# Sum jobs on two hardware queues, raw weights loaded two steps ahead, and a new order in the cosine stage

## The chip, the cores and the metric

The kernel runs on one core of a Trainium2 chip. A core has a matrix engine (TensorE, PE in the profile; its weight loads are PEld), three engines for elementwise work (VectorE, DVE; ScalarE, ACT; GpSimd, POOL), a queue engine (SyncE, SP), and 16 DMA engines between its memory and the chip's. Each engine works through its own list of instructions in order and waits on semaphores. DMAs are started by an instruction on SP, ACT or POOL. The metric is the device time of one execution in microseconds (us).

## The reference

float32, with 2304 tokens (4 x 576), width 512:

```python
x = attention(q, k, v)        # 8 heads of 64; 4 with a window of 32, 4 with 32 positions at a stride of 4
h = x @ w_in                  # 512 -> 2048
r = np.maximum(h, 0.0)
x = (s * (r * r) + b) @ w_out # 2048 -> 512
h = x @ w2_in                 # 512 -> 2048
g = h * np.cos(h)
out = g @ w2_out              # 2048 -> 512
```

## The kernel before

**Numbers.** A float32 factor is split into a high part, rounded to what a fast matmul takes, and the low rest; a product is three matmuls (high x high, high x low, low x high). Splitting is one copy on ACT and one subtraction on DVE. The weights come in as 64-bit words and are converted to float32 on the chip (ACT `w_float`, DVE `w_join`).

**First MLP.** The tokens form five tiles (384, 384, 512, 512, 512). A step `p` is one tile t and one of 16 chunks of 128 of the 2048 hidden columns. In it PE computes the chunk's h (`mm_in`, 12 matmuls from the second tile on), ACT the squared relu, DVE the split g, and PE adds the chunk of two steps before to the output (`mm_out`, 12 matmuls; `LAG` is 2). Attention for later tiles, the conversion of the second MLP's weights and the jobs below are hung into the steps as events: `at((step, phase), ...)`, with `fire` called at three phases of a step. The engines' lists are written in exactly this program order.

**Weights of the second MLP.** 32 pieces are loaded raw (`w2_load`, SP), converted (`w2_float`, `w2_join`) and put back to memory (`w2_cut`): the 16 pieces of w2_out whole, the 16 of w2_in as high and low.

**Jobs.** The last product uses a two-by-two scheme with seven products (M1 to M7), for which the quarters of w2_out have to be combined first. This is done in eight jobs, from step 3 of the last tile on, each one and a half steps after the one before: `job_load` fetches two pieces (two DMAs of 256 KB), `job_sums` makes four sums on DVE, `job_split` splits the seven blocks (two ACT copies, two DVE subtractions) and stores them (two DMAs of 512 KB, two of 384 KB, in pieces of 1 KB). There are two buffers for jobs. Before the change all six DMAs of a job are issued by POOL.

**Second MLP.** It runs over 48 chunk steps n (three splits i of 768 tokens by 16 chunks). In a step PE computes the chunk's h into one of three banks (`mm_h`, 24 matmuls); then come `cos_n` (ACT), `cos_r` and `cos_q` (DVE; one part on ACT in later steps), and `cos_s` (ACT) and `cos_g` (DVE), which end the step before's chunk and so free its bank. `x_cut` splits a quarter of the next split's x. G is combined in place for the seven products; a unit (i, product, k) is 12 matmuls on a split operand (`unit_cut`) with loaded weights (`unit_load`). Units run one in steps 6, 10, 14, 18 and two in each of 27 later steps; the last 26 run after the last chunk. `evacuate` takes a finished product out of its bank.

Of the kernel before, what the change touches and what calls it, by code (L numbers as in the profile page):

```python
# [74 lines left out]
def attention_then_two_mlps(ctx, tc, qk_p, qk_d, v_p, v_d, mask_p, mask_d, w1, w2, sv, bv, out):  # L75
# [134 lines left out]
    def job_load(i):  # L210
        a = after_att[0].tile([P, 7, 256], F32, tag=f"job{i % 2}", name=f"job{i}")
        two = lambda fc: whole_out[fc].rearrange("p (e n) -> p e n", e=2)
        nc.gpsimd.dma_start(a[:, 0:6:5, :], two(2 * i))
        nc.gpsimd.dma_start(a[:, 4:7:2, :], two(2 * i + 1))
        jobs[i] = a
# [6 lines left out]
    def job_split(i):  # L222
        a = jobs.pop(i)
        for n, (lo, hi) in enumerate(((0, 4), (4, 7))):
            h, l = (
                wpool.tile([P, hi - lo, 256], F32R, tag=f"w{c}{2 * (i % 2) + n}", name=f"j{c}{i}_{n}") for c in "hl"
            )
            nc.scalar.copy(h, a[:, lo:hi, :])
            nc.vector.tensor_tensor(out=l, in0=a[:, lo:hi, :], in1=h.bitcast(F32), op=ALU.subtract)  # L229
            nc.gpsimd.dma_start(cut_out[:, lo:hi, i, 0, :], h.bitcast(F32))  # L230
            nc.gpsimd.dma_start(cut_out[:, lo:hi, i, 1, :], l.bitcast(F32))

# [360 lines left out]
    def unit_cut(u):  # L593
# [6 lines left out]
        split[u] = x  # L600
        if j == "M5" and not last:
            t2 = G[i, 0, k][:, 1]
            sub(t2, G[i, 1, k][:, 1], t2)
            ops[i, k, "M6"] = t2
            b11 = G[i, 0, k][:, 0]
            sub(b11, t2, b11)
            ops[i, k, "M7"] = b11
        if j == "M2" and last:
            t2 = home[0].tile([P, 2, SB], F32, tag=f"G{1 - i % 2}0{k}", name=f"t2_{k}")
            sub(t2, G[i, 1, k][:, 1], G[i, 0, k][:, 1])  # L610
            ops[i, k, "M6"] = t2
            b11 = G[i, 0, k][:, 0]
            sub(b11, t2, b11)
            ops[i, k, "M7"] = b11
        if j == "M2":
            b21 = G[i, 1, k][:, 0]
            sub(b21, b21, ops[i, k, "M6"])
            ops[i, k, "M4"] = b21

# [3 lines left out]
    def y_bank(i, j):  # L623
        if i < NS - 1 or j in ("M1", "M6", "M5", "M3"):
            if j in ("M1", "M2", "M7"):
                yy[i, "a"] = ps_o.tile([P, 2, 512], F32, tag="yy", name=f"yy{i}_{j}")
            return yy[i, "a"]
        if j in ("M2", "M7", "M4"):
            b = ps_h.tile([P, 2, 512], F32, tag=f"p{('M2', 'M7', 'M4').index(j) % 2}", name=f"yy{i}_{j}") if j != "M4" else (
                ps_o.tile([P, 2, 512], F32, tag="p2", name=f"yy{i}_{j}"))  # L630
            yy[i, j] = b
        return yy[i, j]
# [45 lines left out]
    def evacuate():  # L678
# [40 lines left out]
    with tc.manual_schedule():  # L719
# [128 lines left out]
        fresh_late = NP - NFC + BG_STEPS[-1][-1] + 2
        for cc in range(NCC):
# [86 lines left out]
        for n in range(1, NH):  # L936
# [119 lines left out]
```

## Time and profile before

| | |
|---|---|
| median of 2 runs | 933.95 us (933.94 to 933.96) |
| profiled execution | 935.2 us, span 933.4 us, granted PE clock 0.98 |
| PE busy | 888.3 us (95%) |
| DVE, ACT, POOL busy | 646.7, 540.9, 39.7 us |
| DMA | 173.09 MB, mean 185 GB/s |

The span is from the first to the last instruction of one profiled execution; its own time is slightly longer, and the median is that of executions without the profiler. A matmul's duration in the rows overlaps that of its neighbours, so the distance of two starts is what one costs. "Idle before <-X" in brackets is how long the engine stood still before the instruction, and what ended it.

### The profile page before, as it was taken

What the parts mean: (1) busy time and instruction counts of PE and PEld (TensorE: products, weight loads), DVE (VectorE), ACT (ScalarE), POOL (GpSimd) and SP (SyncE); (2) the same over time, 40 slices, a digit from 0 to 9 for tenths busy, and PEclk for the clock granted to TensorE, in tenths of its full rate; (3) what the DMA queues carried; (4) which work ended last, traced back from release to release, by engine and by line L of the source; (5) the groups of instructions that cost most, each with busy time, mean ns of one, the idle gap of its engine ahead of it and who ended that gap; (6) DMA issues with size and microseconds to landing.
All of it is one profiled execution on the core that took longest, in us unless ns stands there. A gap on an engine that the chain in (4) does not pass through costs nothing.

```text
span 933.4 us, 13908 instructions
## 1 busy us (share of the span) xinstructions
PE 888.3 (95%) x5148; PEld 788.6 (84%) x5148; DVE 646.7 (69%) x1063; ACT 540.9 (58%) x1079; POOL 39.7 (4%) x58
## 2 busy tenths in 40 slices
PE   8999999999999999999947979989999999999798
PEld 6666699998888888888836779989999999999798
DVE  6888887756554766768634459778677677666954
ACT  6777767766555555655423346546675666655533
POOL 1000000000000000100233300000000000000000
PEclk9999999999999999999978889999999999999999
DMA  9966235324533445456856594355666665665576
GB/s 261 335 235 208 70 123 152 95 96 151 166 119 114 165 165 178 136 185 226 311 214 202 190 351 147 113 181 179 183 199 212 196 183 183 203 212 157 172 243 207
DMA packets 62356, 173.09 MB, mean 185 GB/s; under 512 B 7153, under 2 KB 16849, under 8 KB 62289
## 3 DMA queue, kind: packets, MB, share of 16 engines
q1 hardware_dynamic: 56768, 153.13, 50.5%
q0 software_dynamic: 5376, 18.88, 5.8%
q8 instruction: 41, 0.67, 0.3%
q14 instruction: 27, 0.21, 0.1%
q10 hardware_dynamic: 144, 0.20, 0.1%
HBM read 135.48 MB, written 36.70 MB: 184 GB/s over the span
## 4 chain that ended last, share of the span: by engine, by line
PE 77%; DVE 8%; issue 6%; DMA 5%; ACT 2%; POOL 1%; SPq 1%; DVEq 0%; POOLq 0%
PE h L534 21%; PE yy_M L645 16%; PE h L425 5%; PE h L427 4%; PE h L426 4%; PE y L440 4%; PE y L441 4%; PE y L442 4%; PE y L437 4%; PE h L419 3%; PE sc L300 3%; DMA job<-whole_out 2%; PE pv L376 2%; PE tp L351 1%; DVE jl L229 1%
## 5 line engine op out<-in xcount | busy, mean ns | idle before, releaser
L534 PE MATMUL h<-x,wi 128*128 128x384 f32 x1152 | 209.8, 339 | 11.2 <-issue 11.2
L534 PEld LDWEIGHTS h<-x,wi 128*128 128x128 f32 x1152 | 203.9, 191 | 12.6 <-issue 12.4
L645 PE MATMUL yy_M<-op,wo 128*128 128x384 f32 x1008 | 183.1, 337 | 6.9 <-DVE op L599 5.0
L645 PEld LDWEIGHTS yy_M<-op,wo 128*128 128x128 f32 x1008 | 176.4, 189 | 9.3 <-DVE op L599 5.9
L440 PE MATMUL y<-g,wh 128*128 128x512 f32 (+1 forms) x256 | 101.5, 396 | 18.9 <-DVE g L497 18.9
L543 ACT ACTIVATE n<-h,pmagic 128x768 f32<-128x768 f32 x48 | 43.3, 902 | 114.7 <-PE h L534 107.1
L441 PE MATMUL y<-g,wh 128*128 128x512 f32 (+1 forms) x256 | 99.6, 389 | 0.2 <-DVE g L498 0.2
L442 PE MATMUL y<-g,wl 128*128 128x512 f32 (+1 forms) x256 | 99.0, 387 | 0.0
L425 PE MATMUL h<-xs,wh 128*128 128x512 f32 (+1 forms) x256 | 98.7, 386 | 0.0
L427 PE MATMUL h<-xs,wl 128*128 128x512 f32 (+1 forms) x256 | 96.4, 376 | 0.0
L426 PE MATMUL h<-xs,wh 128*128 128x512 f32 (+1 forms) x256 | 96.3, 376 | 0.0
L552 DVE SCALAR_TENSOR_TENSOR r<-n,h 128x768 f32<-128x768 f32 x48 | 45.8, 953 | 59.5 <-ACT n L548 51.8
L599 DVE TENSOR_TENSOR op<-G,op 128x768 fp32r<-128x768 f32 x80 | 74.4, 952 | 14.5 <-ACT op L598 14.5
L330 ACT ACTIVATE sm<-sm,nmax 96x80 f32<-96x80 f32 (+1 forms) x140 | 49.5, 355 | 49.5 <-DVE nmax L327 49.5
L598 ACT CAST op<-G 128x768 fp32r<-128x768 f32 x80 | 63.7, 828 | 22.5 <-PE yy_M L645 19.5
L440 PEld LDWEIGHTS y<-g,wh 128*128 128x128 f32 x256 | 50.1, 196 | 28.2 <-DVE g L497 20.6
L489 ACT ACTIVATE r<-h 128x512 f32<-128x512 f32 (+1 forms) x80 | 44.0, 550 | 45.2 <-PE h L427 40.3
L497 DVE CAST g<-r 128x512 fp32r<-128x512 f32 (+1 forms) x64 | 26.1, 407 | 51.9 <-ACT r L495 46.2
L570 DVE SCALAR_TENSOR_TENSOR G<-n,h 128x768 f32<-128x768 f32 x48 | 45.7, 953 | 19.5 <-ACT n L562 19.4
L441 PEld LDWEIGHTS y<-g,wh 128*128 128x128 f32 x256 | 49.9, 195 | 9.6 <-DVE g L498 1.9
L442 PEld LDWEIGHTS y<-g,wl 128*128 128x128 f32 x256 | 49.9, 195 | 8.0
L425 PEld LDWEIGHTS h<-xs,wh 128*128 128x128 f32 x256 | 48.1, 188 | 7.8
(108 smaller groups left out, 1323.9 us busy)
## 6 DMA issues: line engine op xcount, KB each, us to landing
wo<-cut_out SPq DMA_DIRECT2D x84, 512.0 KB, 4.2
wi<-cut_in SPq DMA_DIRECT2D x48, 512.0 KB, 5.3
stage<-w SPq DMA_DIRECT2D x32, 512.0 KB, 7.6
raw<-w SPq DMA_DIRECT2D x32, 512.0 KB, 5.0
qk<-qk_d SPq DMA_DIRECT2D x20, 352.0 KB, 3.4
qk<-qk_p SPq DMA_DIRECT2D x20, 304.0 KB, 3.1
x<-y SPq DMA_DIRECT2D x12, 384.0 KB, 6.2
out_t<-o SPq DMA_DIRECT2D x11, 384.0 KB, 3.0
```

Of the source, the lines that this page charges most:

```text
L330: nc.scalar.activation(out=sm[:, j, :], in_=sm[:, j, :], func=AF.Exp, bias=nmax[:, j : j + 1], scale=1.0, accum_out=ssum[:, j : j + 1],)
L425: nc.tensor.matmul(h[:, : SIZES[t]], hi, x[:, 0, :], start=cc == 0, stop=False)
L426: nc.tensor.matmul(h[:, : SIZES[t]], hi, x[:, 1, :], start=False, stop=False)
L427: nc.tensor.matmul(h[:, : SIZES[t]], lo, x[:, 0, :], start=False, stop=cc == NCC - 1)
L440: nc.tensor.matmul(y[:, : SIZES[t]], hi, g[:, 0, :], start=fc == 0, stop=False)
L441: nc.tensor.matmul(y[:, : SIZES[t]], hi, g[:, 1, :], start=False, stop=False)
L442: nc.tensor.matmul(y[:, : SIZES[t]], lo, g[:, 0, :], start=False, stop=fc == NFC - 1)
L534: nc.tensor.matmul(h[:, t, :SB], wt, x[:, t * SB : (t + 1) * SB], start=cc == 0 and k == 0, stop=cc == NCC - 1 and k == 2,)
L552: nc.vector.scalar_tensor_tensor(out=r, in0=v, scalar=-C1, in1=hp[n], op0=ALU.mult, op1=ALU.add)
L598: nc.scalar.copy(x[:, 0], src)
L599: nc.vector.tensor_tensor(out=x[:, 1], in0=src, in1=x[:, 0].bitcast(F32), op=ALU.subtract)
L645: nc.tensor.matmul(b[:, eb, :SB], wt, g, start=fresh and k == 0 and z == 0 and n == 0, stop=k == 3 and z == 1 and n == 2, skip_group_check ...
```

## The change

It moves the job's loads to SP, puts the stores of high parts on ACT and those of low parts on SP, and lets the load of job i + 2 follow the split of job i. Raw weights from the fifth piece on are loaded two steps ahead (phase 1) instead of one (phase 0). The three in-place sums of a split of G come one at a time, kept in a list `due` that `flush` works off later. In the last split the units of M1 and M2 are interleaved. From step 19 on a step first ends the chunk before (`cos_s`, `cos_g`, sums, `x_cut`) and then begins its own cosine. `x_cut` is in other steps, and operands are split as far ahead as the next steps' units need.

```diff
-LAST = ("M1", "M2", "M6", "M7", "M5", "M4", "M3")
+LAST = [("M1", k) for k in "012"] + [("M2", "0"), ("M2", "1"), ("M1", "3"), ("M2", "2"), ("M2", "3")]
+LAST += [(j, k) for j in ("M6", "M7", "M5", "M4", "M3") for k in "0123"]
...
     def job_load(i):
-        nc.gpsimd.dma_start(a[:, 0:6:5, :], two(2 * i))
-        nc.gpsimd.dma_start(a[:, 4:7:2, :], two(2 * i + 1))
+        nc.sync.dma_start(a[:, 0:6:5, :], two(2 * i))
+        nc.sync.dma_start(a[:, 4:7:2, :], two(2 * i + 1))
...
     def job_split(i):
-            nc.gpsimd.dma_start(cut_out[:, lo:hi, i, 0, :], h.bitcast(F32))
-            nc.gpsimd.dma_start(cut_out[:, lo:hi, i, 1, :], l.bitcast(F32))
+            nc.scalar.dma_start(cut_out[:, lo:hi, i, 0, :], h.bitcast(F32))
+            nc.sync.dma_start(cut_out[:, lo:hi, i, 1, :], l.bitcast(F32))
...
     def unit_cut(u):
-        if j == "M5" and not last:
-            t2 = G[i, 0, k][:, 1]
-            sub(t2, G[i, 1, k][:, 1], t2)
-            ops[i, k, "M6"] = t2
-            b11 = G[i, 0, k][:, 0]
-            sub(b11, t2, b11)
-            ops[i, k, "M7"] = b11
...
+        if j == ("M2" if last else "M5"):
+            due.append(lambda: sum_2(i, k))
+        if j == "M6":
+            due.append(lambda: sum_3(i, k))
+        if j == ("M7" if last else "M2"):
+            due.append(lambda: sum_4(i, k))
...
+    def flush():
+        while due:
+            due.pop(0)()
...
             elif j == "M5":
                 keep(i, "v", b)
-                sub(s["v"], s["v"], s["s"])
             elif j == "M6":
                 keep(i, "r", b)
+                sub(s["v"], s["v"], s["s"])
...
-            at((p - 1, 0), lambda k=k: w2_load(k))
+            at((p - 1, 0) if k < BG[1] else (p - 2, 1), lambda k=k: w2_load(k))
...
-            at((max(p - 2, NP - NFC), 2), lambda i=i: job_load(i))
+            if i < 2:
+                at((NP - NFC, 2), lambda i=i: job_load(i))
             at((p, 2), lambda i=i: job_sums(i))
             at((p + 1, 1), lambda i=i: job_split(i))
+            if i + 2 < NFC // 2:
+                at((p + 1, 2), lambda i=i: job_load(i + 2))
...
-        x_at = {5: (1, 0), 7: (1, 1), 9: (1, 2), 11: (1, 3), 22: (2, 0), 24: (2, 1), 26: (2, 2), 28: (2, 3)}
+        x_at = {6: (1, 0), 10: (1, 1), 12: (1, 2), 14: (1, 3), 24: (2, 0), 28: (2, 1), 29: (2, 2), 30: (2, 3)}
...
-            cos_n(n)
-            cos_r(n, n > 17)
-            cos_s(n - 1)
-            cos_g(n - 1)
-            cos_q(n)
-            if n in x_at:
-                x_cut(*x_at[n])
+            if n > 18:
+                cos_s(n - 1)
+                cos_g(n - 1)
+                flush()
+                if n in x_at:
+                    x_cut(*x_at[n])
+                cos_n(n)
+                cos_r(n, True)
+                cos_q(n)
+            else:
+                cos_n(n)
+                cos_r(n, n == 18)
+                cos_s(n - 1)
+                cos_g(n - 1)
+                cos_q(n)
+                flush()
+                if n in x_at:
+                    x_cut(*x_at[n])
...
-            cut_to(nu + 2)
+            ahead = at_unit.get(n + 1, 0)
+            cut_to(nu + ahead + (at_unit.get(n + 2, 0) if ahead < 2 else max(0, n + 3 - NH)))
...
         while nu < len(UNITS):
...
             evacuate()
+            cut_to(nu + 2)
+            flush()
             cut_to(nu + 3)
```

The order of the instructions at three places, before and in the change. Line numbers of the change are one or more higher. First the jobs: POOL's list around the load of the third job before (`job` is a job's buffer, `jh` and `jl` its high and low parts, `cut_out` the store).

```order
L213 DMA job_4501<-whole_out_111 128x2x256
L214 DMA job_4501<-whole_out_112 128x2x256
L230 DMA cut_out<-jh_0_4594 128x4x256
L231 DMA cut_out<-jl_0_4595 128x4x256
L230 DMA cut_out<-jh_1_4600 128x3x256
L231 DMA cut_out<-jl_1_4601 128x3x256
L213 DMA job_4610<-whole_out_113 128x2x256
L214 DMA job_4610<-whole_out_114 128x2x256
```

In the change SP's list at the stores of the third job's low parts and behind them.

```order
L232 DMA cut_out<-jl_0_4649 128x4x256
L232 DMA cut_out<-jl_1_4655 128x3x256
L214 DMA job_4660<-whole_out_115 128x2x256
L215 DMA job_4660<-whole_out_116 128x2x256
L517 DMA x_0_1_4703<-y_0_88 128x768
L517 DMA x_1_1_4706<-y_0_88 128x768
L517 DMA x_2_1_4709<-y_0_88 128x768
L517 DMA x_3_1_4712<-y_0_88 128x768
L232 DMA cut_out<-jl_0_4746 128x4x256
L232 DMA cut_out<-jl_1_4752 128x3x256
```

And ACT's list in the change at the fourth job, with the squared relu of steps 9 and 10 on either side.

```order
L490 ACTIVATE r_9_4727<-h_9_4714 128x512
L496 ACTIVATE r_9_4727<-r_9_4727 128x512
L229 CAST jh_0_4745<-job_4606 128x1024
L231 DMA cut_out<-jh_0_4745 128x4x256
L229 CAST jh_1_4751<-job_4606 128x768
L231 DMA cut_out<-jh_1_4751 128x3x256
L522 CAST x_0_0_4702<-x_0_1_4703 128x768
L490 ACTIVATE r_10_4779<-h_10_4766 128x512
```

The job's DMAs have moved from a list of their own into those of SP, among the loads, and of ACT, between casts and relus.

The second place is DVE's list at chunk steps 7 and 8 before (`n`, `r`: the cosine's tiles by chunk; `G`: the finished chunk; `op`: a split operand).

```order
L550 TENSOR_SCALAR n_7_5397<-n_7_5397 128x768
L552 SCALAR_TENSOR_TENSOR r_7_5400<-n_7_5397,h_7_5370 128x768
L570 SCALAR_TENSOR_TENSOR G_0_1_5313<-n_6_5345,h_6_5318 128x2x384
L580 TENSOR_TENSOR G_0_1_5313<-G_0_1_5313 128x768
L557 SCALAR_TENSOR_TENSOR n_7_5397<-n_7_5397,r_7_5400 128x768
L522 TENSOR_TENSOR x_1_1_5222<-x_1_1_5222,x_1_0_5221 128x768
L599 TENSOR_TENSOR op_5409<-G_0_1_5313,op_5409 128x768
L550 TENSOR_SCALAR n_8_5439<-n_8_5439 128x768
L552 SCALAR_TENSOR_TENSOR r_8_5442<-n_8_5439,h_8_5412 128x768
L570 SCALAR_TENSOR_TENSOR G_1_1_5352<-n_7_5397,h_7_5370 128x2x384
```

In the change:

```order
L551 TENSOR_SCALAR n_7_5397<-n_7_5397 128x768
L553 SCALAR_TENSOR_TENSOR r_7_5400<-n_7_5397,h_7_5370 128x768
L571 SCALAR_TENSOR_TENSOR G_0_1_5313<-n_6_5343,h_6_5316 128x2x384
L581 TENSOR_TENSOR G_0_1_5313<-G_0_1_5313 128x768
L558 SCALAR_TENSOR_TENSOR n_7_5397<-n_7_5397,r_7_5400 128x768
L551 TENSOR_SCALAR n_8_5434<-n_8_5434 128x768
L553 SCALAR_TENSOR_TENSOR r_8_5437<-n_8_5434,h_8_5407 128x768
L571 SCALAR_TENSOR_TENSOR G_1_1_5350<-n_7_5397,h_7_5370 128x2x384
L558 SCALAR_TENSOR_TENSOR n_8_5434<-n_8_5434,r_8_5437 128x768
L601 TENSOR_TENSOR op_5443<-G_0_1_5313,op_5443 128x768
```

The x part (L522) has left step 7, and the split (L599, L601 in the change) stands one step later.

The third place is DVE's list at the last chunk, 47, before (`t`: the sums of the last split).

```order
L552 SCALAR_TENSOR_TENSOR r_47_7900<-n_47_7897,h_47_7869 128x768
L570 SCALAR_TENSOR_TENSOR G_0_3_7763<-n_46_7825,h_46_7800 128x2x384
L580 TENSOR_TENSOR G_0_3_7763<-G_0_3_7763 128x768
L557 SCALAR_TENSOR_TENSOR n_47_7897<-n_47_7897,r_47_7900 128x768
L599 TENSOR_TENSOR op_7936<-G_0_2_7471,op_7936 128x768
L599 TENSOR_TENSOR op_7939<-G_0_3_7763,op_7939 128x768
L570 SCALAR_TENSOR_TENSOR G_1_3_7832<-n_47_7897,h_47_7869 128x2x384
L599 TENSOR_TENSOR op_7945<-G_1_0_6956,op_7945 128x768
L580 TENSOR_TENSOR t_0_7948<-G_1_0_6956,G_0_0_6919 128x768
L580 TENSOR_TENSOR G_0_0_6919<-t_0_7948,G_0_0_6919 128x768
L580 TENSOR_TENSOR G_1_0_6956<-G_1_0_6956,t_0_7948 128x768
L599 TENSOR_TENSOR op_7966<-G_1_1_7252,op_7966 128x768
```

In the change:

```order
L571 SCALAR_TENSOR_TENSOR G_0_3_7758<-n_46_7829,h_46_7800 128x2x384
L581 TENSOR_TENSOR G_0_3_7758<-G_0_3_7758 128x768
L553 SCALAR_TENSOR_TENSOR r_47_7907<-n_47_7904,h_47_7872 128x768
L558 SCALAR_TENSOR_TENSOR n_47_7904<-n_47_7904,r_47_7907 128x768
L571 SCALAR_TENSOR_TENSOR G_1_3_7827<-n_47_7904,h_47_7872 128x2x384
L601 TENSOR_TENSOR op_7942<-G_1_0_6951,op_7942 128x768
L601 TENSOR_TENSOR op_7945<-G_1_1_7244,op_7945 128x768
L581 TENSOR_TENSOR t_0_7962<-G_1_0_6951,G_0_0_6914 128x768
L581 TENSOR_TENSOR t_1_7964<-G_1_1_7244,G_0_1_7171 128x768
L601 TENSOR_TENSOR op_7966<-G_0_3_7758,op_7966 128x768
L601 TENSOR_TENSOR op_7984<-G_1_2_7538,op_7984 128x768
L581 TENSOR_TENSOR t_2_8001<-G_1_2_7538,G_0_2_7464 128x768
```

The G of chunk 46 stands in front of the cosine of chunk 47, and of the sums only `t` is left between the splits.

## Rows read from the trace of the kernel before

**Rows 1.** The page, section 1: busy time, share and instructions by engine.

```profile
PE 888.3 (95%) x5148; PEld 788.6 (84%) x5148; DVE 646.7 (69%) x1063; ACT 540.9 (58%) x1079; POOL 39.7 (4%) x58
```

**Rows 2.** Windows: length; PE, PEld, DVE, ACT, POOL busy; clock, DMA share, GB/s.

```profile
440.00:460.00 20.00, 20.00 (x90) 16.57 (x89) 18.16 (x32) 12.13 (x19) 6.03 (x8) 1.00 0.79 260
...
489.10:532.40 43.30, 36.09 (x133) 28.58 (x134) 22.25 (x36) 15.22 (x23) 15.22 (x21) 0.82 0.55 184
632.00:862.50 230.50, 229.23 (x1321) 228.50 (x1320) 165.86 (x183) 144.45 (x179) 0.00 (x0) 1.00 0.62 193
...
456.00:460.00 4.00, 4.00 (x19) 1.00 0.88 222
```

**Rows 3.** Timeline of PE, last tile: start, us, line, tiles; idle before.

```profile
466.39 0.39 PE L425 MATMUL h<-xs,wh 128*128 128x512 f32 x1
...
468.88 0.39 PE L427 MATMUL h<-xs,wl 128*128 128x512 f32 x1
476.37 0.79 PE L440 MATMUL y<-g,wh 128*128 128x512 f32 x1 [7.10 <-DVE g L497]
...
532.26 16.93 PE L534 MATMUL h<-x,wi 128*128 128x384 f32 x96
```

**Rows 4.** Waits: sum in us, count, longest in us.

```profile
PE y L440 <- DVE g L497: 18.9, 4, 7.1
...
ACT n L543 <- DMA cut_out<-jh: 7.6, 1, 7.6
```

**Rows 5.** Timeline of POOL at the third job.

```profile
482.21 0.73 POOL L213 DMA_DIRECT2D job<-whole_out  x1 [0.49 <-issue]
...
485.84 0.77 POOL L230 DMA_DIRECT2D cut_out<-jh  x1 [2.18 <-issue]
489.54 0.77 POOL L231 DMA_DIRECT2D cut_out<-jl  x1 [2.93 <-DVE g L497]
...
494.55 0.74 POOL L213 DMA_DIRECT2D job<-whole_out  x1 [0.53 <-issue]
```

**Rows 6.** DMA issues (KB, median us to landing); landings of L230.

```profile
y<-xy SPq DMA_DIRECT2D x2, 512.0 KB, 4.1
...
DMA to landing us min/median/max: 3.4/3.9/10.3
```

**Rows 7.** Timeline of SP and ACT queues: DMA issues.

```profile
418.51 1.21 SPq L462 DMA_DIRECT2D y<-xy  x2
...
548.13 7.37 SPq L516 DMA_DIRECT2D x<-y  x4
...
930.01 0.37 ACTq L669 DMA_DIRECT2D out_t<-o  x1
```

**Rows 8.** Chain of waits: start, us, what (`issue`: PE stands still).

```profile
549.21 5.31 issue
554.52 10.82 PE h L534 x48
...
579.93 1.29 issue
...
620.52 3.27 issue
...
631.87 4.16 PE h L534 x24
```

**Rows 9.** Timeline of DVE before the G at 580.18.

```profile
576.92 0.95 DVE L522 TENSOR_TENSOR x<-x,x 128x768 fp32r<-128x768 f32 x1
...
578.65 0.55 DVE L550 TENSOR_SCALAR n<-n 128x768 f32<-128x768 f32 x1
...
580.18 0.95 DVE L570 SCALAR_TENSOR_TENSOR G<-n,h 128x768 f32<-128x768 f32 x1
```

**Rows 10.** Chain of waits: PE's last chunk and last products.

```profile
858.36 4.17 PE h L534 x24
...
904.25 25.22 PE yy_M L645 x144
```

More of the change, by code (lines that the diff above doesn't have):

```diff
@@ L580, in sub @@
         nc.vector.tensor_tensor(out=out, in0=a, in1=b, op=ALU.subtract)
-    UNITS = [(i, j, k) for i in range(NS) for j in (PRODUCTS if i < NS - 1 else LAST) for k in range(4)]
+    UNITS = [(i, j, k) for i in range(NS - 1) for j in PRODUCTS for k in range(4)]
+    UNITS += [(NS - 1, j, int(k)) for j, k in LAST]
     cutn = [0]
@@ L600, in unit_cut, with sum_2, sum_3, sum_4 @@
         split[u] = x
-        if j == "M5" and not last:
-            t2 = G[i, 0, k][:, 1]
-            sub(t2, G[i, 1, k][:, 1], t2)
-            ops[i, k, "M6"] = t2
-            b11 = G[i, 0, k][:, 0]
-            sub(b11, t2, b11)
-            ops[i, k, "M7"] = b11
-        if j == "M2" and last:
-            t2 = home[0].tile([P, 2, SB], F32, tag=f"G{1 - i % 2}0{k}", name=f"t2_{k}")
[L610 to L618, printed above, removed]
+        if j == ("M2" if last else "M5"):
[4 more added lines that the diff above has]
+            due.append(lambda: sum_4(i, k))
+    due = []
+    def flush():
+        while due:
+            due.pop(0)()
+    def sum_2(i, k):
+        t2 = G[i, 0, k][:, 1]
+        if i == NS - 1:
+            t2 = home[0].tile([P, 2, SB], F32, tag=f"G{1 - i % 2}0{k}", name=f"t2_{k}")
+        sub(t2, G[i, 1, k][:, 1], G[i, 0, k][:, 1])
+        ops[i, k, "M6"] = t2
+    def sum_3(i, k):
+        b11 = G[i, 0, k][:, 0]
+        sub(b11, ops[i, k, "M6"], b11)
+        ops[i, k, "M7"] = b11
+    def sum_4(i, k):
+        b21 = G[i, 1, k][:, 0]
+        sub(b21, b21, ops[i, k, "M6"])
+        ops[i, k, "M4"] = b21
     yy = {}
@@ L623, in y_bank @@
     def y_bank(i, j):
[L624 to L632, printed above, removed]
+        if j in ("M5", "M6", "M3") or (j == "M4" and i < NS - 1):
+            return yy[i, "M7" if j == "M4" else "M1"]
+        place, tag = (ps_o, "yy")
+        if i == NS - 1 and j != "M1":
+            place, tag = {"M2": (ps_h, "p0"), "M7": (ps_h, "p1"), "M4": (ps_o, "p2")}[j]
+        return place.tile([P, 2, 512], F32, tag=tag, name=f"yy{i}_{j}")
     def unit(u):
@@ L636, in unit @@
         if k == 0:
-            yy[i, "now"] = y_bank(i, j)
-        b = yy[i, "now"]
+            yy[i, j] = y_bank(i, j)
+        b = yy[i, j]
         fresh = j in ("M1", "M2", "M7") or (i == NS - 1 and j == "M4")
@@ L683, in evacuate @@
         if i < NS - 1:
-            b = yy[i, "a"][:, :, :SB]
+            b = yy[i, j][:, :, :SB]
             if j == "M1":
@@ L701, in evacuate @@
             return
-        b = yy[i, "now"][:, :, :SB]
+        b = yy[i, j][:, :, :SB]
         if j == "M1":
```

## The prediction

> **What bounds the kernel now.** I read the page first: TensorE (PE) counts as busy for 95% of the span [rows 1], so a change can win little more than the idle remainder and what a lowered clock adds to it. Busy time by stretch comes next [rows 2]: from 632 to 862 us PE is busy 229.23 of 230.50 us at full clock, and nothing but PE counts there. In the last tile of the first MLP it is busy 36.09 of 43.30 us (489.1 to 532.4) at a granted clock of 0.82. Third I read PE's timeline and the waits [rows 3, 4]. The reader should see PE stop at 468.88 + 0.23 and start again at 476.37, waiting for DVE's g: four such waits, 18.9 us. DVE is idle then too; it stands in front of the sums of a job, whose raw weights are not yet loaded. POOL's timeline shows why [rows 5]: it issues loads and stores of the jobs one at a time, a store's two issues 3.70 us apart (485.84 to 489.54), and a job's six DMAs take 12.34 us (482.21 to 494.55). PE gives a job one and a half steps; from 466.39 to 468.88 eleven matmul starts take 2.49 us, so 0.227 us each, 24 matmuls and 5.44 us a step, **8.16 us** a job. POOL is the slower of the two, and the DMA engines are busy only 0.55 there [rows 2].
>
> **The sum, stretch by stretch.** The profiled execution's span is 933.4 us, its own time 935.2; the median of the runs, 933.95, is 0.55 above the span. I subtract from the span and add 0.55.
>
> *A, last tile, 469.1 to 532.4 us.* PE has left there seven output groups and four input groups of 12 matmuls (11 x 2.72 = 29.9 us) and one cosine chunk of 24 (4.16 us, [rows 8]): 34.1 us of work in 63.3 us [rows 3]. With the jobs off POOL up to **29.2 us** can go, slow-clock time included, since the difference is taken against full-speed work.
> What replaces it: 16 job loads and 16 stores of the low halves on SP, 16 stores of the high halves on ACT. Issue: the nearest row is the parked y, also 512 KB in pieces of 1 KB, 1.21 us for two on SP; the ends are 0.37 us (ACT's one store) and 1.84 us (four x loads in 7.37 us when the engines are full) [rows 7]. I take 0.6, by likeness: 1.2 us a job on ACT, 2.4 on SP. ACT is busy 15.22 of 43.30 us there [rows 2], 4.3 us per 12.34 us job, so 5.5 of 8.16 with the stores: hidden by PE. If that cover went, 8 x 1.2 = 10 us would show.
> On SP the job's load now stands behind the low stores of the job two before it, and these wait for DVE; behind them wait x and w_in loads. The load goes out about two steps (10.9 us) ahead of its sums, against landings of 3.9 median and 10.3 longest for POOL's stores and 4.1 for the parked y [rows 6]. So it lands just in time even in the longest case.
> Bytes: a job moves 2 x 256 + 2 x 512 + 2 x 384 KB = 2.36 MB. At 184 GB/s for a share of 0.55 the engines carry about 334 GB/s when full, an estimate from that row, so 7.1 us a job: under 8.16, not far. Jobs 3 to 7, four x and four w_in loads are 15.5 MB, 46.3 us, while steps 8 to 15 last 43.5. I therefore leave 3 us in (bounds 0 to 18, see the first rival): **-26.2**.
> DVE was the tightest engine before step 8 (18.16 of 20.00 us busy at 440 to 460, [rows 2]); nothing is added to it, and PE did not stall while it was so.
> A rule of the Trainium skill, "DMA: Bandwidth & Descriptors", section "Issuing engines are not separate DMA queues", speaks against this term: all queues share the same 16 engines, and issuing from several saves only issue time, which is usually small beside the transfer. The trace differs: engines at 0.55 while POOL paces them. By the rule the time would be that of the third rival, 918; by the row it is the one here.
>
> *B, 549.2 to 554.5 us.* PE waits 5.31 us for a bank [rows 8]; the cosine that frees it waited 7.6 us for the last job's store to leave its memory [rows 4]. Now that store goes out in step 15, before PE's last two output groups. The chain from the first cosine chunk to its freed bank is some 9 us and PE has three chunks (12.5 us) to do: **-5.3** (0 if the stores land 5 us late).
>
> *C, chunks 5 to 18, 554.5 to 631.9 us.* 77.35 us for 384 matmuls [rows 8] of 4.16/24 = 0.173 us: 66.6 us of work, 10.8 lost. One part is the slow clock after B's stop (48 matmuls in 10.82 instead of 8.32). The rest comes from three stops, two of 1.29 and one of 3.27 us: a chunk's bank is freed by DVE's G, and in the step before the G at 580.18 DVE also had a difference, an x part and a split to do [rows 9]. The change spreads them: x parts move to steps 6, 10, 12 and 14, three of which also run a product on PE (2.08 us more cover); splits move by one; the two in-place sums of a split leave step 15. A step has four fixed DVE instructions, 0.55 and three of 0.95 [rows 9], 3.4 of 4.16 us; one more of 0.95 now fits before the bank is due. I leave 1.8 us for steps with two extras: **-9.0** (bounds -10.8 to 0).
>
> *D, 632 to 862 us.* Doing a step's end before the new chunk's cosine moves DVE's G out from behind the wait for PE, but PE hardly waits: at most 1.27 us [rows 2]. I take **-0.6**. The move of one difference from M5 to M6 and the later sums cost nothing here: 8.32 us of PE a step cover them; without that cover it is the second rival.
>
> *E, the end.* From 862.53 to 929.47 us [rows 10] PE runs 28 products of 12 matmuls, 58.2 us at 0.173: 8.7 lost, most of it waiting for operands that DVE had not split. Three sums per M2 split (0.95 each) sat in DVE between two splits. Now the last G but one no longer waits for the last chunk, three M1 and two M2 products come before the late M1 product, and each split has one sum behind it: 1.9 us of DVE for 2.08 of PE. Following the new order, the first M2 split still comes about 1 us late, and two more about 0.5 each: 2 us stay, **-6.7** (bounds -8.7 to 0).
>
> *Weights two steps ahead.* The last 28 of the 32 raw loads go out more than a step earlier. Where the tile before them was stored in place, SP now waits for that store to land, and what is queued behind it (q and k loads, the next store) with it; these have whole steps of PE's work ahead of them. No wait of PE's names a raw load, so there is nothing to win or to lose: 0. Without that cover it would show as waits for g before step 8.
>
> Sum: 26.2 + 5.3 + 9.0 + 0.6 + 6.7 = 47.8; 933.4 - 47.8 + 0.55 = **886 us**. A measurement of this kernel can tell about 2% (19 us) from no change.
>
> **Rivals.**
> 1. *The DMA engines take POOL's place.* For: 15.5 MB against 43.5 us leaves nothing over, and at 456 to 460 us a share of 0.88 moved only 222 GB/s [rows 2], 252 at full share. Then the stretch takes 61.5 us, 18 more; PE's lag of two steps hides some of it at the end. With 15 us the time is **901**. Against: the y row's 4.1 us, as fast as POOL's stores. Chance 0.14.
> 2. *DVE becomes the bound in the 27 chunk steps with two products.* If each loses what D's two gaps show (1.27/2 = 0.64 us), that is 17 us: **903**. For: G, a sum, an x part, r, q and two splits follow one another there. Against: seven such instructions are 6.7 of 8.32 us. Chance 0.08.
> 3. *The jobs keep their pace* on the new queues, because each still waits for the one before: A and B stay, and 16.3 us are won: **918**. Against: the loads are ahead by two steps and the engines are free for 0.45 of the time. Chance 0.06.
> 4. *Slower: ACT is held by its own stores.* The built program gives its hardware-queue DMAs eight semaphores in turn, so a store on ACT can wait for the DMA eight before it to land, and ACT's relu, and with it g and PE, stand behind it. ACT's own work is 4.3 us a job; if a store holds it for its landing, a median of 3.9 makes 12.1 us a job, today's pace, which is the third rival. It turns slower by 2% when jobs take (18.7 + 16.3)/7 = 5.0 us more than 12.34, which is a hold of **6.5 us** a store. At the longest landing of 10.3 [rows 6] a job takes 24.9 us: 7 x 12.6 - 16.3 = +72, **1006**. Against: 0.37 us for ACT's one store. Chance 0.03.
>
> **Chances and range.** The forecast has 0.63, with its own range of 880 (all bounds: 29.2 + 5.3 + 10.8 + 1.27 + 8.7 = 55.3 won, less the 2 us that the new end keeps) to 893; the rest, 0.06, are partial wins between 893 and 915. To leave out no more than 2 in 10 the range reaches to the first two rivals: 880 to 903. Faster by over 2% (below 915): 0.91; within 2%: 0.06; slower: 0.03.
>
> **What would show it.** Right: PE without a wait for g from step 12 on, clock 1.00 through the last tile, a job every 8.2 us, no stop at the fifth chunk, none of 1.29 us before chunks 10, 14 and 18, and 60 to 61 us from the last chunk to the last product. Wrong in A: DVE's sums still waiting for a job's load, with the DMA share near 1.00 (first rival) or near 0.6 (third), or ACT's stores with us-long issue times (fourth). Wrong in D: PE below 229 of 230 us.

## Result and profile after

The changed kernel takes **882.13 us** (881.93 to 882.33), the ratio to before is **0.9445**, 95% interval [0.9405, 0.9486]. The forecast was 886, its range 880 to 903. The profiled execution took 881.93 us, its span is 880.1 us, its granted clock 1.00.

The line of the page that answers to [rows 1]:

```profile
PE 871.9 (99%) x5148; PEld 778.9 (88%) x5148; DVE 647.0 (74%) x1063; ACT 545.1 (62%) x1079; POOL 3.5 (0%) x10
```

The windows of the changed kernel, with the columns of [rows 2]: before step 8, the last tile, chunks 5 to 18, the steps up to the last chunk, the end.

```profile
440.00:460.00 20.00, 20.00 (x90) 16.57 (x89) 18.00 (x32) 12.28 (x19) 0.00 (x0) 1.00 0.87 291
466.20:503.20 37.00, 37.00 (x170) 31.39 (x169) 25.29 (x41) 18.95 (x26) 0.00 (x0) 1.00 1.06 376
520.00:587.50 67.50, 67.50 (x388) 66.86 (x386) 58.51 (x71) 44.54 (x55) 0.00 (x0) 1.00 0.51 173
587.50:816.40 228.90, 228.90 (x1322) 228.90 (x1322) 169.32 (x188) 148.83 (x181) 0.00 (x0) 1.00 0.63 195
816.40:876.20 59.80, 58.93 (x336) 57.88 (x335) 40.71 (x45) 26.26 (x32) 0.00 (x0) 1.00 0.75 238
```

PE is busy throughout until the last chunk is done; the clock does not fall. The engine that is full now is the DMA engines' group: share 1.06 and 376 GB/s in the last tile, where [rows 2] had 0.55 and 184. The chain of waits (start, us, what) gives the landmarks to set against [rows 8, 10]. The first line is chunk 1 in the kernel before, the others are the changed kernel:

```profile
532.43 16.78 PE h L534 x96
```

```profile
503.22 25.44 PE h L535 x144
...
585.41 2.08 PE yy_M L655 x12
...
812.22 4.17 PE h L535 x24
...
823.93 52.27 PE yy_M L655 x299
```

The x144 are chunks 1 to 6, so chunk 5 starts at 503.22 + 96/144 x 25.44 = 520.18. Where the 53.3 us of span went:

| stretch | before, us | after, us | gained | forecast |
|---|---|---|---|---|
| A: last tile, from the h matmuls at 466 to chunk 1 (466.39 to 532.43; 466.18 to 503.22) | 66.04 | 37.04 | 29.0 | 26.2 |
| B: chunks 1 to 4 (to 554.52; to 520.18) | 22.09 | 16.96 | 5.1 | 5.3 |
| C: chunks 5 to 18 (to 631.87; to 587.49) | 77.35 | 67.31 | 10.0 | 9.0 |
| D: to the end of the last chunk (862.53; 816.39) | 230.66 | 228.90 | 1.8 | 0.6 |
| E: to the last product (929.47; 876.20) | 66.94 | 59.81 | 7.1 | 6.7 |

What is left of PE's waits (us in total, times, longest):

```profile
PE keep L485 <- DVE g L476: 1.4, 1, 1.4
PE yy_M L655 <- DVE op L601: 0.7, 1, 0.7
```

No wait for g is left after the start, and none for a bank. What the jobs do in the last tile, on ACT (a store takes 0.37 to 0.45 us there):

```profile
454.64 1.05 ACT L229 CAST jh<-job 128x1024 fp32r<-128x1024 f32 x1 [0.76 <-DVE job L221]
...
463.56 0.84 ACT L229 CAST jh<-job 128x768 fp32r<-128x768 f32 x1 [0.59 <-DVE g L499]
466.69 0.42 ACTq L231 DMA_DIRECT2D cut_out<-jh  x1
470.36 0.83 ACT L522 CAST x<-x 128x768 fp32r<-128x768 f32 x1 [5.96 <-DMA x<-y]
...
490.67 0.60 ACT L490 ACTIVATE r<-h 128x512 f32<-128x512 f32 x1 [1.48 <-DMA cut_out<-jl]
...
494.40 1.05 ACT L229 CAST jh<-job 128x1024 fp32r<-128x1024 f32 x1 [1.32 <-DVE job L221]
```

Five jobs lie between 454.64 and 494.40, 7.95 us each, close to PE's 8.16 and no longer POOL's 12.34. ACT stands still twice for long. From 464.40 (463.56 + 0.84) to 466.69 it is held in front of a store, then until 470.36 it waits for an x part that the full engines bring late; the 5.96 us of the row count both. Before 490.67 a relu comes 1.48 us late and the row names the landing of a store that SP issued: the store in front of it on ACT was held for that landing. This is what the fourth rival described, twice and for some 3 us in all, and PE has no wait for g from it. The landings (KB, median us) are longer than the 3.9 us that the working took from [rows 6]:

```profile
job<-whole_out SPq DMA_DIRECT2D x16, 256.0 KB, 5.5
cut_out<-jh ACTq DMA_DIRECT2D x8, 512.0 KB, 5.5
cut_out<-jl SPq DMA_DIRECT2D x8, 512.0 KB, 7.6
```

So a job's load still comes late at times. DVE's waits for one (us in total, times, longest), before and in the change:

```profile
DVE job L220 <- DMA job<-whole_out: 41.8, 6, 14.7
```

```profile
DVE job L221 <- DMA job<-whole_out: 6.2, 3, 4.0
```

### The profile page after: what moved, and what is told of

Read it like the earlier page. It is cut to its first block, busy times and chain, and to the rows that moved or that the text cites. A ratio compares the mean times of both kernels' runs of the same rounds, so it can differ in the third digit from the quotient of the medians.

```text
span 880.1 us, 13889 instructions
## 1 busy us (share of the span) xinstructions
PE 871.9 (99%) x5148; PEld 778.9 (88%) x5148; DVE 647.0 (74%) x1063; ACT 545.1 (62%) x1079; POOL 3.5 (0%) x10
## 4 chain that ended last, share of the span: by engine, by line
PE 93%; DVE 3%; DMA 2%; ACT 1%; SPq 1%; issue 0%; DVEq 0%
PE h L535 23%; PE yy_M L655 19%; PE h L426 6%; PE h L428 6%; PE h L427 6%; PE y L441 6%; PE y L443 6%; PE y L442 6%; PE y L438 4%; PE h L420 4%; PE sc L301 3%; PE pv L377 2%; PE tp L352 1%; DMA first_v<-v_d 1%; DVE wa L152 1%; DMA first_v<-v_p 1%
## 5 line engine op out<-in xcount | busy, mean ns | idle before, releaser
L535 PE MATMUL h<-x,wi 128*128 128x384 f32 x1152 | 205.9, 335 | 0.0
L535 PEld LDWEIGHTS h<-x,wi 128*128 128x128 f32 x1152 | 200.6, 188 | 0.8 <-issue 0.6
L655 PE MATMUL yy_M<-op,wo 128*128 128x384 f32 x1008 | 180.6, 335 | 0.9 <-DVE op L601 0.7
L441 PE MATMUL y<-g,wh 128*128 128x512 f32 (+1 forms) x256 | 97.7, 382 | 0.0
L443 PE MATMUL y<-g,wl 128*128 128x512 f32 (+1 forms) x256 | 96.2, 376 | 0.0
L442 PE MATMUL y<-g,wh 128*128 128x512 f32 (+1 forms) x256 | 96.1, 375 | 0.0
L601 DVE TENSOR_TENSOR op<-G,op 128x768 fp32r<-128x768 f32 x80 | 73.7, 952 | 9.3 <-ACT op L600 9.2
L426 PEld LDWEIGHTS h<-xs,wh 128*128 128x128 f32 x256 | 48.1, 188 | 7.8
L428 PEld LDWEIGHTS h<-xs,wl 128*128 128x128 f32 x256 | 48.0, 188 | 7.6
L443 PEld LDWEIGHTS y<-g,wl 128*128 128x128 f32 x256 | 48.0, 188 | 7.5
L427 PEld LDWEIGHTS h<-xs,wh 128*128 128x128 f32 x256 | 48.1, 188 | 7.3
```

The source lines that it names most:

```text
L426: nc.tensor.matmul(h[:, : SIZES[t]], hi, x[:, 0, :], start=cc == 0, stop=False)
L427: nc.tensor.matmul(h[:, : SIZES[t]], hi, x[:, 1, :], start=False, stop=False)
L428: nc.tensor.matmul(h[:, : SIZES[t]], lo, x[:, 0, :], start=False, stop=cc == NCC - 1)
L441: nc.tensor.matmul(y[:, : SIZES[t]], hi, g[:, 0, :], start=fc == 0, stop=False)
L442: nc.tensor.matmul(y[:, : SIZES[t]], hi, g[:, 1, :], start=False, stop=False)
L443: nc.tensor.matmul(y[:, : SIZES[t]], lo, g[:, 0, :], start=False, stop=fc == NFC - 1)
```

## Experiments

Times are medians; the ratio to the kernel before follows with its 95% interval. Theory: POOL's pace made A and B, and DVE's order in the cosine stage made C, D and E, each a sum of its own. First rival: other parts of the change share the gain in A (earlier loads, the weights two steps ahead).

**The queues alone, in the kernel before**

```diff
-        nc.gpsimd.dma_start(a[:, 0:6:5, :], two(2 * i))
+        nc.sync.dma_start(a[:, 0:6:5, :], two(2 * i))
...
-            nc.gpsimd.dma_start(cut_out[:, lo:hi, i, 0, :], h.bitcast(F32))
-            nc.gpsimd.dma_start(cut_out[:, lo:hi, i, 1, :], l.bitcast(F32))
+            nc.scalar.dma_start(cut_out[:, lo:hi, i, 0, :], h.bitcast(F32))
+            nc.sync.dma_start(cut_out[:, lo:hi, i, 1, :], l.bitcast(F32))
```

> The kernel before with one edit: job loads on SP, stores of high parts on ACT, of low parts on SP. Everything else is as before. Theory (POOL's issue pace was the bound of the last tile, and nothing else of the change acts there): the terms A and B go whole, 29.0 + 5.1 us by the two traces, 933.95 - 34.1 = 900 us, and C, D and E stay. Rival 1 (the gain in A also needs the raw weights two steps ahead or the new place of the loads): about 910 to 920, with DVE's sums waiting for a job's load. Rival 2 (what the last tile gains is lost again at the start of the cosine): 905 to 930, with a wait at the fifth chunk.

900.51 us, 0.9643 [0.9625, 0.9662]: the theory's 900. The three stops of C stand in its chain of waits, as in [rows 8]:

```profile
545.95 1.30 issue
...
566.25 1.30 issue
...
586.56 3.27 issue
589.84 5.99 PE h L534 x24
```

C takes 75.0 us here (522.87 to 597.90), 2.3 less than before: that part of C was the slow clock behind B's stop (granted clock 0.78 from 554.5 to 565.3 before, 1.00 from 522.8 to 533.6 here), and belongs to the queues. The other 7.7 belong to the cosine's order. Behind the stop of 3.27 us the clock falls here too (24 matmuls in 5.99 us).

The first rival holds for a small part. Chunk 1 starts at 505.75 here, 532.26 before and 503.06 in the changed kernel (PE's timeline): of 29.2 us the queues alone give 26.5, the earlier loads and raw weights the other 2.7 (raw weights some 1.1, below; the earlier loads were not tried alone).

**The queues undone, in the changed kernel**

```diff
-        nc.sync.dma_start(a[:, 0:6:5, :], two(2 * i))
+        nc.gpsimd.dma_start(a[:, 0:6:5, :], two(2 * i))
...
-            nc.scalar.dma_start(cut_out[:, lo:hi, i, 0, :], h.bitcast(F32))
-            nc.sync.dma_start(cut_out[:, lo:hi, i, 1, :], l.bitcast(F32))
+            nc.gpsimd.dma_start(cut_out[:, lo:hi, i, 0, :], h.bitcast(F32))
+            nc.gpsimd.dma_start(cut_out[:, lo:hi, i, 1, :], l.bitcast(F32))
```

> The changed kernel with the jobs' six DMAs put back on POOL, the rest of the change kept. Theory: A and B come back, 882.1 + 34.1 = 916 us, clock below 1.00 in the last tile, four waits for g. Rival 1 (part of A came from the earlier loads): 900 to 910. Rival 2 (the rest of the change needs a full clock or an early start of the cosine): more than 925.

916.16 us, 0.9817 [0.9802, 0.9832]. The two halves add up: 933.73 - 900.51 = 33.2 us by the queues alone, 933.73 - 916.16 = 17.6 by the rest, 50.8 of the 51.8 together. A window of its last tile (columns of [rows 2]):

```profile
466.30:528.40 62.10, 47.18 (x170) 36.54 (x170) 29.49 (x49) 19.95 (x28) 20.74 (x28) 0.84 0.57 197
```

The same 170 matmuls, 62.1 us at a clock of 0.84 and a share of 0.57, 3.9 us less than before.

**Only the loads off POOL, in the kernel before**

```diff
-        nc.gpsimd.dma_start(a[:, 0:6:5, :], two(2 * i))
-        nc.gpsimd.dma_start(a[:, 4:7:2, :], two(2 * i + 1))
+        nc.sync.dma_start(a[:, 0:6:5, :], two(2 * i))
+        nc.sync.dma_start(a[:, 4:7:2, :], two(2 * i + 1))
```

> The kernel before with the jobs' two loads on SP and all four stores left on POOL. It parts two ways in which POOL can pace. Theory 1 (POOL spends time on every 1 KB piece: a job is 512 pieces of loads and 1792 of stores in 12.34 us, 5.4 ns each): stores alone take 1792 x 5.4 ns = 9.6 us a job against PE's 8.16, so 7 x 1.4 = 10 us of A's 29 stay and some of B: 908 to 915 us. Theory 2 (POOL paces because a job's loads stand in one list behind stores that wait for DVE): with the loads out of that list the pace is PE's, 900 us. Theory 3 (the stores alone hold the pace): 930 or more.

920.69 us, 0.9866 [0.9847, 0.9885]: below all of theory 3, above theory 1's range. Chunk 1 starts at 516.90 on PE's timeline, 13.8 us later than in the changed kernel and 15.4 earlier than before; B stays whole. Its timeline, of POOL, of ACT, of DVE and of PE in turn:

```profile
494.29 0.88 POOL L230 DMA_DIRECT2D cut_out<-jh  x1
501.79 0.77 POOL L231 DMA_DIRECT2D cut_out<-jl  x1 [6.62 <-issue]
```

```profile
503.47 0.83 ACT L228 CAST jh<-job 128x768 fp32r<-128x768 f32 x1 [9.00 <-DMA cut_out<-jh]
```

```profile
501.57 1.23 DVE L229 TENSOR_TENSOR jl<-job,jh 128x1024 fp32r<-128x1024 f32 x1 [5.91 <-DMA cut_out<-jl]
```

```profile
504.85 6.75 PE L534 MATMUL h<-x,wi 128*128 128x384 f32 x24 [4.75 <-ACT r L489]
```

POOL puts 6.62 us between two stores with nothing shown that it waits for; the split two jobs later then waits for its buffer to be stored, on ACT and DVE, and relu and g stand behind it. So the stores alone still hold the pace, 13.8 / 7 = 2.0 us a job over PE's 8.16; the price by pieces, 9.6 us a job, gave 1.4. Two windows between stores (columns of [rows 2]) show why that price is no constant:

```profile
494.29:501.79 7.50, 4.88 (x12) 3.32 (x12) 1.55 (x4) 0.18 (x1) 0.88 (x3) 0.77 0.98 325
503.71:507.39 3.68, 2.54 (x8) 2.54 (x9) 2.13 (x4) 2.83 (x5) 0.76 (x2) 0.50 0.56 197
```

The second is the 3.70 us of [rows 5] again, at a DMA share of 0.56. In the first the DMA engines are full, and POOL's next store comes 7.50 us after the one before, though DVE had finished that store's data at 480.35. DVE is busy for only 1.55 us of the window, so it isn't DVE's work that holds POOL up. That the full engines do is likely from these two windows; no run parts it from other causes.

**Only the loads back on POOL, in the changed kernel**

```diff
-        nc.sync.dma_start(a[:, 0:6:5, :], two(2 * i))
-        nc.sync.dma_start(a[:, 4:7:2, :], two(2 * i + 1))
+        nc.gpsimd.dma_start(a[:, 0:6:5, :], two(2 * i))
+        nc.gpsimd.dma_start(a[:, 4:7:2, :], two(2 * i + 1))
```

> The changed kernel with only the jobs' two loads put back on POOL, the stores staying on ACT and SP. Theory (the stores set POOL's pace, loads_off_pool having taken only 13 of 34 us off with them still there): POOL then issues two loads of 0.73 us in 8.16 us, nothing waits: 882 to 883 us. Rival (a job's load needs a hardware queue): 890 to 900 us, with DVE's sums waiting for it.

882.86 us, 0.9454 [0.9436, 0.9472]: nothing lost. The stores are what had to leave POOL; two loads a job may stay.

**All six DMAs of a job on SP, in the changed kernel**

```diff
-            nc.scalar.dma_start(cut_out[:, lo:hi, i, 0, :], h.bitcast(F32))
+            nc.sync.dma_start(cut_out[:, lo:hi, i, 0, :], h.bitcast(F32))
```

> The changed kernel with the stores of high parts on SP too, so that one hardware queue issues all six DMAs of a job. Theory (the second queue is not needed): in the changed kernel an issue on SP took 0.4 to 1.6 us there; six are 5 to 7 us of the 8.16 us that PE gives a job, hidden: 882 to 885 us. Rival (SP becomes what POOL was): six issues at 1.26 us, the x and w_in loads and the waits for DVE make 9 to 10 us a job, 7 x 1 to 2 us: 890 to 897, with DVE's sums waiting for the load.

882.22 us, 0.9456 [0.944, 0.9473]. One job on SP's timeline:

```profile
474.46 0.80 SPq L231 DMA_DIRECT2D cut_out<-jh  x1
...
480.15 1.11 SPq L215 DMA_DIRECT2D job<-whole_out  x1
```

All six go out in 6.8 us from the start of the first to the end of the last, against 12.34 on POOL from a job's first to the next job's first [rows 5]. The number of hardware queues is worth nothing here; that the stores are on one is worth the 33 us of the queues.

**Every store of low parts twice, in the changed kernel**

```diff
+            for _ in range(2):
-            nc.sync.dma_start(cut_out[:, lo:hi, i, 1, :], l.bitcast(F32))
+                nc.sync.dma_start(cut_out[:, lo:hi, i, 1, :], l.bitcast(F32))
```

> The changed kernel with every store of low parts issued twice, the same data to the same place, which adds 8 x (512 + 384) KB = 7.3 MB to the jobs. It asks how near the DMA engines stand to being the bound (the first rival of the prediction). In the changed kernel they move 376 GB/s at a share of 1.06 in the last tile. Theory (they are full and only just hidden): 7.3 MB at 376 GB/s are 19.5 us, of which some 2 to 5 are covered: 897 to 900 us, with PE waiting for g and DVE for the jobs' loads or for stores to leave their memory. Rival (there is slack, the full share is transfers put early): 882 to 886.

926.23 us, 0.992 [0.9898, 0.9942], far from both. It did not measure what it was for. A row of SP's waits (us in total, times, longest), one of its timeline, and a window (columns of [rows 2]):

```profile
SPq L233 <- DMA cut_out<-jl: 74.0, 16, 6.9
```

```profile
485.61 13.09 SPq L233 DMA_DIRECT2D cut_out<-jl  x4
```

```profile
480.00:500.00 20.00, 11.14 (x39) 8.38 (x38) 7.85 (x12) 7.54 (x11) 0.00 (x0) 0.74 0.89 297
```

The second store goes to the place of the first, and the built program has SP wait for the first one's semaphore before it: 16 waits, one for each second store, 4.6 us on average and up to 6.9. The next job's load stands behind them. This is a wait in the program, not one that the chip added. The engines carry less than in the changed kernel (297 against 376 GB/s), so 44 us are the price of a queue that is held for landings, not of 7.3 MB. How much more the engines could have carried stays open.

**Raw weights one step ahead, in the changed kernel**

```diff
-            at((p - 1, 0) if k < BG[1] else (p - 2, 1), lambda k=k: w2_load(k))
+            at((p - 1, 0), lambda k=k: w2_load(k))
```

> The changed kernel with the raw weights of the second MLP loaded one step ahead again. Theory of the prediction (no wait of PE's names a raw load, so the earlier loads are worth nothing): 882.1 us. Rival (with the jobs' loads and stores on SP a raw load stands behind them and comes late): in the run queues_alone, which has the old place of the raw loads, ACT's conversion waited 4.02 us for one and PE reached the last tile's first stretch about 0.7 us and the stretch after it a further 1.0 us later than in the changed kernel; so 883 to 884.5 us, with ACT waiting for raw weights near 450 us.

883.93 us, 0.9477 [0.9462, 0.9492], the rival's side, though the intervals overlap. ACT's wait for raw weights, first as one row, then as the sum here and in the changed kernel:

```profile
450.24 0.67 ACT L138 ACTIVATE wa<-raw 128x512 f32<-128x512 f32 x1 [3.66 <-DMA raw<-w]
```

```profile
ACT wa L138 <- DMA raw<-w: 7.9, 5, 3.7
```

```profile
ACT wa L138 <- DMA raw<-w: 1.4, 1, 1.4
```

PE runs the last tile at the same times as in the changed kernel up to 458.02 us, waits there and once more for g (0.2 us idle each time, 0.4 in all), and is 1.12 us later at chunk 1: some 1.1 us. So the rival's mechanism is shown by the trace, and the times agree with it.

**Old places of x parts and splits, in the changed kernel**

```diff
-        x_at = {6: (1, 0), 10: (1, 1), 12: (1, 2), 14: (1, 3), 24: (2, 0), 28: (2, 1), 29: (2, 2), 30: (2, 3)}
+        x_at = {5: (1, 0), 7: (1, 1), 9: (1, 2), 11: (1, 3), 22: (2, 0), 24: (2, 1), 26: (2, 2), 28: (2, 3)}
...
-            ahead = at_unit.get(n + 1, 0)
-            cut_to(nu + ahead + (at_unit.get(n + 2, 0) if ahead < 2 else max(0, n + 3 - NH)))
+            cut_to(nu + 2)
```

> The changed kernel with the x parts in their old chunk steps and operands split only two units ahead. Theory (C's gain has two causes: places, which take the two stops of 1.29 us before chunks 10 and 14, and the put-off sums, which take the stop of 3.27 us before chunk 18): the two small stops come back and the late splits cost about 1 us at the end: 884.5 to 886.5 us. Rival (places alone make all that C and E give at full clock, 7.7 + about 3 us): 890 to 893.

885.41 us, 0.9495 [0.9478, 0.9512]. The stops are back, three of them, and the one of 3.27 us has become one of 1.29:

```profile
543.45 1.29 issue
...
584.03 1.29 issue
585.32 4.43 PE h L535 x24
```

C takes 4.1 us more (520.37 to 591.83). But the end takes 0.8 us less (820.73 to 879.73, 59.00 us): there the expectation had the wrong sign.

**The in-place sums at once, in the changed kernel**

```diff
-            due.append(lambda: sum_2(i, k))
-        if j == "M6":
-            due.append(lambda: sum_3(i, k))
-        if j == ("M7" if last else "M2"):
-            due.append(lambda: sum_4(i, k))
+            sum_2(i, k)
+            sum_3(i, k)
+        if j == "M2":
+            sum_4(i, k)
```

> The changed kernel with the in-place sums of a split done at once behind it, as before. Theory (the sums behind one split are what stops PE before chunk 18 and between the M2 products of the end): 3.3 us in C and up to 2 sums x 0.9 us x 3 splits = 5 us at the end: 886 to 890 us. Rival (the new places of the splits give the sums room, so they cost nothing at once either): 882 to 883.

888.54 us, 0.9526 [0.9512, 0.9541], the theory's range, but not as it was split up: the stretch from chunk 5 to the last chunk takes 1.7 us more (520.36 to 818.23), not 3.3, and the end 4.7 more (818.23 to 882.79). All of the 1.7 lies in D: C takes 67.3 us, as in the changed kernel, and the stop of 3.27 us before chunk 18, which the theory gave to the sums, does not come back. The waits and a piece of the chain at the end:

```profile
PE yy_M L654 <- DVE op L601: 5.4, 6, 1.2
```

```profile
828.46 0.87 DVE op L601
829.32 0.88 DVE t L581
830.23 1.83 DVE G L581 x2
```

Three sums, 2.7 us of DVE, behind one split, for 2.1 us of PE.

**The old order of the last split's products, in the changed kernel**

```diff
-LAST = [("M1", k) for k in "012"] + [("M2", "0"), ("M2", "1"), ("M1", "3"), ("M2", "2"), ("M2", "3")]
-LAST += [(j, k) for j in ("M6", "M7", "M5", "M4", "M3") for k in "0123"]
+LAST = [(j, k) for j in ("M1", "M2", "M6", "M7", "M5", "M4", "M3") for k in "0123"]
```

> The changed kernel with the products of the last split in their old order, M1 whole, then M2. Theory (the end gained from sums one at a time and from G ahead of the cosine, and the interleaving only covers the last chunk's cosine): PE has four M1 products, 8.3 us, while the last cosine's chain takes 7.5 us, so the old order costs 0 to 2 us: 882 to 884. Rival (the interleaving is what took the waits out of the end): most of the 7.1 us come back, 887 to 889.

882.44 us, 0.9459 [0.9444, 0.9473]; the end takes 59.7 us (817.05 to 876.72). The interleaving is worth nothing.

**A step's own cosine first again, in the changed kernel**

```diff
-            if n > 18:
+            if n > NH:
...
-                cos_r(n, n == 18)
+                cos_r(n, n > 17)
```

> The changed kernel with every step beginning its own cosine before it ends the chunk before, as before the change. Theory (D's gain, 230.66 - 228.90 = 1.8 us between the nineteenth chunk and the last, comes from this order): 1.3 to 1.8 us come back there and up to 1 us at the end: 883.5 to 885 us. Rival 1 (it comes from the splits further ahead, and the order is worth nothing): 882. Rival 2 (the order carries the end too, because the G of chunk 46 again waits for the cosine of chunk 47): 887 or more.

890.73 us, 0.9541 [0.9521, 0.9561]: in the range of the second rival, and a miss of the theory. Of the rival's mechanism, a longer end, only 2.4 us are there: the end takes 62.2. D takes 234.0 us (588.42 to 822.47), 5.1 more than in the changed kernel and 3.4 more than even the kernel before. The first line is a stop of D in the kernel before; then come PE's and DVE's timeline here:

```profile
703.23 4.40 PE L645 MATMUL yy_M<-op,wo 128*128 128x384 f32 x24 [0.64 <-issue]
```

```profile
660.65 4.40 PE L655 MATMUL yy_M<-op,wo 128*128 128x384 f32 x24 [1.50 <-ACT n L544]
678.17 4.40 PE L655 MATMUL yy_M<-op,wo 128*128 128x384 f32 x24 [0.64 <-issue]
```

```profile
656.13 1.82 DVE L581 TENSOR_TENSOR G<-G,G 128x768 f32<-128x768 f32 x2
657.86 1.82 DVE L601 TENSOR_TENSOR op<-G,op 128x768 fp32r<-128x768 f32 x2
659.60 0.95 DVE L685 SCALAR_TENSOR_TENSOR o<-yy_M,s 128x768 f32<-128x768 f32 x1
```

The two stops that D had before (0.64 us each, 71.4 and 88.9 us behind the start of D) stand in the same two steps again (72.2 and 89.8 us behind it), the first now 1.50 us long, and two more have come (0.53 and 1.49). The profile puts PE's longest wait down to ACT's `n`, but a new product starts there, and PE goes on 0.1 us after `o` (L685, 659.60 + 0.95) has emptied the product's bank. `o` stands behind two sums and two splits, which stand behind a G that waited for the new chunk's cosine. The places of sums and splits in the change fit only the new order.

**One split ahead of the last chunk's G, in the changed kernel**

```diff
-            cut_to(nu + ahead + (at_unit.get(n + 2, 0) if ahead < 2 else max(0, n + 3 - NH)))
+            cut_to(nu + ahead + (at_unit.get(n + 2, 0) if ahead < 2 else max(0, n + 3 - NH)) if n < NH - 1 else nu + 2)
```

> The changed kernel with one operand split put ahead of the last chunk's G instead of behind it. In old_places, which has the split there, the last stretch took 59.00 us, in the changed kernel 59.81, with one wait of 0.7 us for a split. Theory: that wait goes, 881.4 us, a difference that the trace should show (59.0 us from the last chunk to the last product) and the times hardly can. Rival: the split delays the last G by as much and the wait only moves, 882.1.

880.74 us (880.44 to 880.97), 0.943 [0.9414, 0.9446]. Its chain of waits at the end:

```profile
812.86 4.16 PE h L535 x24
817.01 58.27 PE yy_M L655 x336
```

28 products in 58.27 us without a gap, 1.5 us less than the changed kernel: the wait of 0.7 us in that kernel was the visible half, since a stop costs more than its idle time (see D below). This version is the fastest of all, by about what the intervals can tell.

## Why the prediction was right

The forecast held for its reasons, 3.9 us too high.

**A, right mechanism, size 2.8 short.** POOL's pace was the bound: its six DMAs undone or done alone are 33 to 34 us of A, B and the clock. I left 3 us in for the DMA engines, and none was lost. Two of my numbers were wrong in opposite directions. The engines' full rate, which I set at 334 GB/s from the share of [rows 2], measured 376 at a share of 1.06, so the bytes fitted. The landings, which I took at 3.9 us, became 5.5 to 7.6, and where I had a job's load land in time even in the longest case, DVE's sums waited for one three times, 6.2 us in all. That is the sign I had set for the first rival, sums waiting for a load with full engines; its price was not paid, because PE adds a chunk to the output two steps later and never waited for g. That these errors cancelled is luck, and no run shows how near the price was. The third rival fell with the job's pace. The fourth rival's hold is there, twice on ACT, and hidden in the same way; a store's own 0.37 us says nothing of it. The doubled store shows what such holds cost where nothing hides them, there by another wait of the program: 44 us.

The Trainium skill, "DMA: Bandwidth & Descriptors", section "Issuing engines are not separate DMA queues", says that issuing from several engines saves only issue time, usually small beside the transfer. One half is borne out: all DMAs on SP alone took 882.22 us, so a second hardware queue saves nothing. The other half does not hold for stores on POOL: there issue set the pace. The same page of the Trainium skill, section "SWDGE vs HWDGE vs iDMA", says that DMAs from GpSimd get their descriptors from software and those from SP and ACT from hardware that is faster to set up. The trace agrees, with 12.34 us on POOL against 6.8 on SP for one job's six.

**B, right.** 5.3 for 5.1.

**C, right.** 9.0 for 10.0; I left 1.8 us in, and 0.7 stayed. Of the 10.0, 2.3 are the slow clock behind B's stop, which came with the queues. Places and sums, which I named together, act together: the places of x parts and splits cost 4.1 when undone alone, the sums undone alone nothing, and both as before (the queues alone) 7.7. The 3.6 between are a third stop that is 2.0 longer and the slow clock behind it, 1.6 (5.99 us instead of 4.43).

**D, mis-sized.** I took PE's idle time from busy sums, at most 1.27 us, and halved it. Both stops went whole. Each was 0.64 us idle, and the 24 matmuls behind it took 4.40 us instead of 4.16, since a matmul's record overlaps the next and this overlap is missing behind a stop. That makes 1.8. The order of a step is what took the stops out: with it undone alone, they stand in the same steps again. I had priced this order at that little. Undone alone it costs 5.1 us in D and 2.4 in E, since the new places of sums and splits lean on it; this is the mechanism of the prediction's second rival, which the change itself did not meet.

**E, right sum, a wrong share.** 6.7 for 7.1. Of the 8.7 us lost there before, some 1.7 were a slow clock, which I had counted in without naming it. The row of the kernel before:

```profile
869.82 12.31 PE L645 MATMUL yy_M<-op,wo 128*128 128x384 f32 x60 [2.56 <-DVE op L599]
```

Behind this wait of 2.56 us the granted clock is 0.86 for these 60 matmuls, 12.31 us instead of some 10.6 (an estimate: 0.173 each, and the 0.24 of D behind a stop). The sums one a split carry most of the gain (4.7 undone alone), the order of a step 2.4. The interleaving of M1 and M2, which I counted among the reasons, does nothing. The first M2 split, which I expected to be late, was, and the two others were not: the run with one split ahead of the last G shows 1.5 us of my 2.

**Weights two steps ahead, off by a little.** I priced them at nothing, since no wait of PE's named a raw load before. On an SP queue that also carries the jobs, a raw load one step ahead comes late, and that costs about 1.1 us.

The sum of the terms was 47.8 of 53.1 us; the median lies 2.0 us above the span here and lay 0.55 above it before, which gave 1.5 us back. This last part is luck too: the profiled execution before was 1.2 us slower than the median.

## What to carry to other kernels

Where one queue issues at a steady pace, idle between issues with nothing to wait for, compare its period with that of the engine it feeds: the ratio is worth more than its busy share, which was 4% here. Moving its stores to a hardware queue that has room gave 33 of the 52 us, and a full group of DMA engines cost nothing here, where loads went out two steps ahead (raw weights one step ahead cost 1.1 us). Orders on an engine are priced together, not one by one: D's whole difference is 1.8 us, and undoing the new order of a step alone cost 8.6.

## Not expected of the hardware

- Six DMAs of 1 KB pieces (2.36 MB) take 12.34 us to issue on POOL and 6.8 on SP. On POOL the issue took longer where the DMA engines were full: from one store to the next 3.68 us at a share of 0.56 (a store of 512 KB), 7.50 at 0.98 (one of 384 KB), both in the run with only the loads off POOL.
- The DMA engines moved 376 GB/s over 37 us at a share of 1.06, while at 0.88 in the kernel before they moved 222 [rows 2]: the share does not measure what is left.
- Behind a stop of PE's of 0.64 us the next 24 matmuls took 4.40 us instead of 4.16 at full clock, so a short stop costs 0.9 us and not what its idle time says.
